# A linear-attention and token-mixing kernel: 20 of its 24 activation transposes moved from TensorE to DMA transposes

## The chip, the cores and the metric

One core of one Trainium2 chip runs the whole kernel. The metric is the device time of one launch in microseconds, lower is better. Five runs of the kernel before gave a median of 159.87 us (157.64 to 160.91).

## What is computed

The reference first runs a decayed linear attention over `r`, `k`, `v` (batch 4, 8 heads, 768 tokens, head width 48), then mixes the result, called x (4 x 768 x 384), across tokens and channels:

```python
for t in range(S):                       # per batch and head
    cur = einsum('bhd,bhe->bhde', u * k[t], v[t])
    y[t] = einsum('bhd,bhde->bhe', r[t], state + cur)
    state = w * state + einsum('bhd,bhe->bhde', k[t], v[t])
...
theta = x @ w_theta
zr, zi = x * cos(theta), x * sin(theta)
u = x + einsum('ts,bsd->btd', w_tok_r, zr) + einsum('ts,bsd->btd', w_tok_i, zi)
out = u + maximum(u @ w_ch, 0)
```

Inputs and output are float32; inside, most products are taken in bfloat16.

## The kernel before

**The work.** The 768 tokens are cut into 6 chunks of 128; two chunks make a pair, and there are 3 pairs in a batch and 12 in all. I call them g0 to g11, g = 3 * batch + pair. The attention is done in chunked form (line 506, `attention`): k is scaled on GpSimd (POOL, L520), turned on TensorE (PE), scored against r (L543), masked on VectorE (DVE, L548); a running state S goes from chunk to chunk (L585, L593, L603, L613); the products with v and with S make y (L627, L632); and DVE adds a diagonal term to give x (L639), token-major, bfloat16, 128 partitions x 768 for a pair.

**The two matrices that are turned.** `theta` (L651) needs x with channels on the partitions, so x of a pair is turned block by block (six 128 x 128 blocks) into xT. ScalarE (ACT) then takes sin (L655) and cos (L658), and DVE and POOL multiply with x to give zr (L661) and zi (L664). When zr and zi of the three pairs of a batch are there, `mixing` (line 668) sums over all tokens: each output chunk takes 12 matmuls, issued as 4 parts of 3 (L683), and DVE adds x to give un (L689). `f` (L700) needs un with channels on the partitions, so un of a pair is turned in the same way into uT; DVE then makes `fin` (L704), and SyncE (SP) stores it (L708).

In the kernel before, `flips` (defined above L473) does both turns: six TensorE transposes against an identity into one PSUM bank (L473), and a copy of the 128 x 768 result into SBUF, on DVE (L261) or ACT (L259). xT, un, uT and fin each have two buffers. The turned r (RT) and k (KT) come from the same helper, and the token weights are turned in fp32 at L456; the change leaves these alone.

**What sets the order.** Nothing is ordered by hand. `P.add` records each task with the engines that may run it, a cost for each as (busy ns, latency ns), its reads and writes, and a priority; `Plan.order` (line 88) then simulates the five engines with these costs, and the order of starts that comes out is the order in which each engine's instructions are issued. Engines run their own list strictly in order. A task with two engines among its options goes where the plan has it done first. DMAs are tasks of SP: loads cost 1080 ns (k, v), 3500 ns (r of a batch) and so on with a latency of 2100 ns and have a priority of -1e6 plus their number; the output stores have (1000, 2000) and a priority of -2e6, ahead of every load that could start at the same moment:

```python
P.add({SP: (ns, 2100)}, lambda e: nc.sync.dma_start(out=dst, in_=src), wr=wr,
      prio=-1e6 + pos, name="load")
```

All loads but three tiny ones, and all stores, go through SP. Loads run ahead into ten staging tiles `ld` and two `r_f` tiles. On SP, a DMA also waits for the DMA issued eight before it, whose semaphore it takes over.

The plan counts PE instructions as `pe_op(ns)`, an extra latency of 215 ns, and a copy as `ev(n)`, ACT or DVE.

Of the kernel before, what the change touches and what calls it, by code (L numbers as in the profile page):

```python
# [16 lines left out]
BF16 = mybir.dt.bfloat16  # L17
# [3 lines left out]
PE, DVE, ACT, POOL, SP = "PE", "DVE", "ACT", "POOL", "SP"  # L21
# [167 lines left out]
def act_op(n, psum=True, ptr=False):  # L189
    return (n / 1.2 + (85 if psum else 100) + (90 if ptr else 0), 135)  # L190


def dve_op(n, rate=1.0):
    return (n / (0.96 * rate) + 70, 115)
# [6 lines left out]
def pe_op(ns):  # L201
    return (ns, 215)


@with_exitstack
def kernel(
    ctx: ExitStack,
    tc: tile.TileContext,
    r: bass.AP,
    k: bass.AP,  # L210
    v: bass.AP,
    w: bass.AP,
    u: bass.AP,
    moe_w_theta: bass.AP,
    moe_w_tok_r: bass.AP,
    moe_w_tok_i: bass.AP,
    moe_w_ch: bass.AP,
    out: bass.AP,
):
    nc = tc.nc  # L220
    P = build(ctx, tc, nc, r, k, v, w, u, moe_w_theta, moe_w_tok_r, moe_w_tok_i, moe_w_ch, out)
    ctx.enter_context(tc.manual_schedule())
    for t in P.order():
        t.fn(t.eng)


def build(ctx, tc, nc, r, k, v, w, u, moe_w_theta, moe_w_tok_r, moe_w_tok_i, moe_w_ch, out):
    B, H, S, D = r.shape
    HD = H * D
    C = 128  # L230
    NCH = S // C
    ND = HD // C
    Dp = 64
    HP = H // 2
    NP = NCH // 2
# [4 lines left out]
    P = Plan(SLOTS)  # L240
    banks = [ps.tile([C, n, 512], F32, name=f"bank{i}") for i, n in enumerate(SLOTS)]

    def dbl(tok):
        return banks[P.bank_of[tok]]

    def bank(tok):
        return banks[P.bank_of[tok]][:, 0]

    def bank16(tok):
        return banks[P.bank_of[tok]].bitcast(BF16)[:, 0]  # L250

    def ring(n, shape, dt, nm):
        return [sb.tile(shape, dt, name=f"{nm}{i}") for i in range(n)]
# [3 lines left out]
    def copy(e, dst, src):  # L257
        if e == ACT:
            nc.scalar.activation(dst, src, Act.Copy)  # L259
        else:  # L260
            eng_of[e].tensor_copy(dst, src)  # L261
# [17 lines left out]
    wS = sb.tile([C, HP, 2 * D], F32, name="wS")  # L279
    uw = sb.tile([C, HP, 2], BF16, name="uw")  # L280

    NL, NR, NK, NV = 10, 2, 4, 5
    Ls = ring(NL, [C, 2, H, Dp], F32, "ld")
    r_fs = ring(NR, [C, H, NCH * D], F32, "r_f")
    Rws = ring(1, [C, NCH, H, Dp], BF16, "Rw")
# [10 lines left out]
    zrs = ring(2, [C, NCH, HD], BF16, "zr")  # L296
    zis = ring(2, [C, NCH, HD], BF16, "zi")
    sins = ring(2, [C, 2, HD], BF16, "sin")
    xTs = ring(2, [C, 2 * ND, C], BF16, "xT")
    uns = ring(2, [C, 2, HD], BF16, "un")  # L300
    uTs = ring(2, [C, 2 * ND, C], BF16, "uT")
    fins = ring(2, [C, 2, HD], F32, "fin")
    Wth = sb.tile([C, ND, HD], BF16, name="Wth")
    Wch = sb.tile([C, ND, HD], BF16, name="Wch")
# [127 lines left out]
    def L2(i):  # L432
        return [("L", i, 0), ("L", i, 1)]
# [34 lines left out]
    def flips(dst, blocks, tok, prio, rd, wr, name, opts, src=lambda t: t):  # L468
        n = len(blocks)

        def go(e):
            for i, s in enumerate(blocks):
                nc.tensor.matmul(bank16(tok)[:, i * C:(i + 1) * C], s, ident,  # L473
                                 is_transpose=True, start=(i == 0), stop=(i == n - 1))
        P.add({PE: pe_op(56 * n)}, go, rd=rd + ["ident"], acq=[(tok, 1)], prio=prio, name=name)
        P.add(opts, lambda e: copy(e, dst, src(
            bank16(tok)[:, :n * C].rearrange("p (a c) -> p a c", a=n))),
            use=[tok], wr=wr, prio=prio, name=name + "ev")

    EV = {ACT: None, DVE: None}  # L480

    def ev(n):
        return {ACT: act_op(n), DVE: dve_op(n, 2.0)}
# [22 lines left out]
    def attention(b, pr, base):  # L506
        RT, x, zr, zi = RTs[b % 2], xs[b % 2], zrs[b % 2], zis[b % 2]
        zj = b % 2
        g = b * NP + pr
        pb = base  # L510
# [13 lines left out]
        if b == 0:  # L524
# [9 lines left out]
            rd=L2(iv) + ["tables done"], wr=[kv_], prio=pb + 1, name="vcast")  # L534

        for c in range(2):
            tk, cc = ("A", g, c), 2 * pr + c

            def scores(e, tk=tk, c=c, cc=cc):
                for hp in range(HP):  # L540
# [6 lines left out]
                  prio=pb + 2, mode=1, name="scores")  # L547
# [7 lines left out]
            rd=[kT] + rt_keys, wr=[kP], prio=pb + 2.5, lock=True, name="PD")  # L555
# [35 lines left out]
        def outer0(e):  # L591
            if S_in:
# [5 lines left out]
              rd=[kK, kv_] + ([S_in, "ident"] if S_in else []), acq=[(tS, 1)], prio=pb + 2.2,  # L598
              name="outer")
# [10 lines left out]
        if not last:  # L610
            P.add({PE: pe_op(170)}, lambda e: outer(1, False), rd=[kK, kv_], use=[tS], wr=[tS],
                  prio=pb + 2.4, name="outer")
# [6 lines left out]
        def outputs(e):  # L619
            for c in range(2):  # L620
# [17 lines left out]
        xk = [("x", zj, pr)]  # L638
# [1 line left out]
            x[:, 2 * pr:2 * pr + 2], dbl(ty)[:, :, :HD], yd),  # L640
            use=[ty], rd=[ky], wr=xk, prio=pb + 5, name="x")

        xT, sn = xTs[g % 2], sins[g % 2]
        flips(xT, [x[:, 2 * pr + t, dk * C:(dk + 1) * C] for t in range(2) for dk in range(ND)],
              ("TX", g), pb + 6, xk, [("xT", g % 2)], "xT", ev(6 * C))
        th = ("th", g)

        def theta(e):
            for t in range(2):
                for dk in range(ND):  # L650
                    nc.tensor.matmul(dbl(th)[:, t, :HD], xT[:, ND * t + dk, :], Wth[:, dk, :],  # L651
                                     start=(dk == 0), stop=(dk == ND - 1))
        P.add({PE: pe_op(980)}, theta, rd=[("xT", g % 2), ("Wth", 0), ("Wth", 2)],
              acq=[(th, 2)], prio=pb + 7, name="theta")
        P.add({ACT: act_op(2 * HD)}, lambda e: nc.scalar.activation(  # L655
            sn, dbl(th)[:, :, :HD], Act.Sin), use=[th], rd=["tables done"],
            wr=[("sin", g % 2)], prio=pb + 7, name="sin")
        P.add({ACT: act_op(2 * HD, True, True)}, lambda e: nc.scalar.activation(  # L658
            dbl(th)[:, :, :HD], dbl(th)[:, :, :HD], Act.Sin, bias=pi2), use=[th],
            wr=[th], rd=["pi2"], prio=pb + 7.1, name="cos")  # L660
        P.add({DVE: dve_op(2 * HD)}, lambda e: nc.vector.tensor_mul(  # L661
            zr[:, 2 * pr:2 * pr + 2], dbl(th)[:, :, :HD], x[:, 2 * pr:2 * pr + 2]), use=[th],
            rd=xk, wr=[("zr", zj, pr)], prio=pb + 8, name="zr")
        P.add({POOL: pool_op(2 * HD, 1.9)}, lambda e: nc.gpsimd.tensor_mul(  # L664
            zi[:, 2 * pr:2 * pr + 2], x[:, 2 * pr:2 * pr + 2], sn),
            rd=xk + [("sin", g % 2)], wr=[("zi", zj, pr)], prio=pb + 8, lock=True, name="zi")

    def mixing(b, pr, base):
        x, zr, zi = xs[b % 2], zrs[b % 2], zis[b % 2]
        zj = b % 2  # L670
        zk = [("zr", zj, o) for o in range(NP)] + [("zi", zj, o) for o in range(NP)]
        g = b * NP + pr
        un, uT, fin = uns[g % 2], uTs[g % 2], fins[g % 2]
        pb = base
        for t in range(2):
            to = 2 * pr + t
            tm = ("mx", b, to)
            for part in range(4):
                def mix(e, tm=tm, to=to, part=part):
                    WT, z = ((WrT, zr), (WiT, zi))[part // 2]  # L680
                    for j in range(3):
                        so = 3 * (part % 2) + j
                        nc.tensor.matmul(bank(tm)[:, :HD], WT[:, so, to * C:(to + 1) * C],  # L683
                                         z[:, so], start=(part == 0 and j == 0),
                                         stop=(part == 3 and j == 2))
                P.add({PE: pe_op(490)}, mix, rd=zk + [(n, to) for n in ("WrT", "WiT")],
                      acq=[(tm, 1)] if part == 0 else [], use=[] if part == 0 else [tm],
                      wr=[] if part == 0 else [tm], prio=pb + t - 0.01 * part, name="mix")
            P.add({DVE: dve_op(HD)}, lambda e, tm=tm, t=t, to=to: nc.vector.tensor_add(  # L689
                un[:, t], bank(tm)[:, :HD], x[:, to]), use=[tm],  # L690
                rd=[("x", zj, pr)], wr=[("un", g % 2, t)], prio=pb + t - 100, name="un")
        flips(uT, [un[:, t, dk * C:(dk + 1) * C] for t in range(2) for dk in range(ND)],
              ("TU", g), pb + 2, [("un", g % 2, t) for t in range(2)], [("uT", g % 2)], "uT",
              ev(6 * C))
        tf = ("f", g)

        def chan(e):
            for t in range(2):
                for dk in range(ND):
                    nc.tensor.matmul(dbl(tf)[:, t, :HD], uT[:, ND * t + dk, :], Wch[:, dk, :],  # L700
                                     start=(dk == 0), stop=(dk == ND - 1))
        P.add({PE: pe_op(980)}, chan, rd=[("uT", g % 2), ("Wch", 0), ("Wch", 2)],
              acq=[(tf, 2)], prio=pb + 2, name="f")
        P.add({DVE: dve_op(2 * HD)}, lambda e: nc.vector.scalar_tensor_tensor(  # L704
            fin, dbl(tf)[:, :, :HD], 0.0, un, op0=Alu.max, op1=Alu.add),
            use=[tf], rd=[("un", g % 2, t) for t in range(2)], wr=[("fin", g % 2)],
            prio=pb - 98, name="fin")
        P.add({SP: (1000, 2000)}, lambda e: nc.sync.dma_start(  # L708
            out=out[b, 2 * pr * C:(2 * pr + 2) * C, :].rearrange("(t p) n -> p t n", p=C),
            in_=fin), rd=[("fin", g % 2)], wr=[("out", g)], prio=-2e6, name="out")  # L710
# [3 lines left out]
    load_r(0, 2)  # L714
    heads(0, 0)
    attention(0, 0, 5)
    attention(0, 1, 15)
    attention(0, 2, 25)
    token_weights(range(0, 3), 40)
    load_r(1)  # L720
# [3 lines left out]
    for b in range(1, B + 1):  # L724
        if b < B:
            if b > 1:
                load_r(b)
                heads(b, 100 * b)
            for pr in range(NP):
                attention(b, pr, 100 * b + 5 + 10 * pr)  # L730
        for pr in range(NP):
            mixing(b - 1, pr, 100 * (b - 1) + 150 + 10 * pr)
# [31 lines left out]
```

## Time and profile before

| what | value |
|---|---|
| median of 5 runs | 159.87 us |
| the profiled execution, its own time | 159.87 us |
| its span in the trace | 158.2 us |
| DVE, ACT, POOL busy | 109.3, 76.5, 75.8 us |
| HBM read, written | 20.06 MB, 4.72 MB |

The span is the stretch that the trace covers; 1.67 us of the execution's time lie outside it. In the profile, a row of a group gives line, engine, operation, output and inputs with their shapes, the count, then busy time in us and the mean ns of one, then how long the engine sat idle just before these instructions and what ended that. "L473 <-ident,x" are the transposes of x, "L473 <-ident,un" those of un. Times of "DMA to landing" run from the issue on SP to the semaphore.

Three parts of the run matter below: the start (to about 42 us: weights, batch 0), the middle (42 to 96 us: batches 1 and 2, while k and v still stream in), and the end (from 96 us: no more loads, only stores).

### The profile page before, as it was taken

What the parts mean: (1) busy time and instruction counts of PE and PEld (TensorE: products, weight loads), DVE (VectorE), ACT (ScalarE), POOL (GpSimd) and SP (SyncE); (2) the same over time, 40 slices, a digit from 0 to 9 for tenths busy, and PEclk for the clock granted to TensorE, in tenths of its full rate; (3) what the DMA queues carried; (4) which work ended last, traced back from release to release, by engine and by line L of the source; (5) the groups of instructions that cost most, each with busy time, mean ns of one, the idle gap of its engine ahead of it and who ended that gap; (6) DMA issues with size and microseconds to landing.
All of it is one profiled execution on the core that took longest, in us unless ns stands there. A gap on an engine that the chain in (4) does not pass through costs nothing.

```text
span 158.2 us, 3653 instructions
## 1 busy us (share of the span) xinstructions
PE 133.7 (85%) x1491; PEld 94.0 (59%) x1491; DVE 109.3 (69%) x158; ACT 76.5 (48%) x119; POOL 75.8 (48%) x61
## 2 busy tenths in 40 slices
PE   4077695599999999999889929999999999999950
PEld 1056564368787767669656717668567676566620
DVE  5196898812723999969999657667996975555540
ACT  3987238349887547558735184516317445000000
POOL 7000731669994846957599766910712442100000
PEclk9999999959999999999999999999999999999995
DMA  4999999999799999999999940202200022021022
GB/s 150 264 227 183 163 276 397 367 393 366 246 180 167 159 205 192 163 160 266 264 192 195 157 77 0 102 9 92 100 3 4 0 102 98 5 99 70 30 99 99
DMA packets 59962, 25.00 MB, mean 158 GB/s; under 512 B 50473, under 2 KB 58410, under 8 KB 59946
## 3 DMA queue, kind: packets, MB, share of 16 engines
q1 hardware_dynamic: 59920, 24.78, 74.5%
q8 instruction: 11, 0.18, 0.6%
q14 instruction: 5, 0.04, 0.1%
q10 hardware_dynamic: 26, 0.00, 0.0%
HBM read 20.06 MB, written 4.72 MB: 157 GB/s over the span
## 4 chain that ended last, share of the span: by engine, by line
PE 56%; DVE 21%; DMA 7%; SPq 7%; issue 3%; ACT 2%; POOL 1%; ACTq 1%; DVEq 0%; POOLq 0%
PE bank L683 23%; PE bank L473 8%; PE bank L700 7%; SPq L404 7%; PE bank L651 5%; DVE mAT L548 5%; PE bank L456 4%; DMA ld<-in_k_dram 4%; DMA ld<-in_v_dram 4%; DVE zr L661 3%; DVE PD L553 2%; PE bank L632 2%; PE bank L543 2%; DVE fin L704 2%; PE bank L627 2%
## 5 line engine op out<-in xcount | busy, mean ns | idle before, releaser
L683 PE MATMUL bank<-zi,WiT 128*128 128x384 bf16 x144 | 29.7, 326 | 0.0
L683 PE MATMUL bank<-zr,WrT 128*128 128x384 bf16 x144 | 29.2, 326 | 0.0
L548 DVE TENSOR_TENSOR mAT<-bank,mask 128x1024 bf16<-128x1024 f32 x24 | 28.8, 1216 | 0.1
L664 POOL TENSOR_TENSOR zi<-x,sin 128x768 bf16<-128x768 bf16 x12 | 20.6, 1720 | 15.7 <-ACT sin L655 15.7
L520 POOL TENSOR_TENSOR Kw<-ld,wpinv 128x768 bf16<-128x768 f32 x10 | 18.6, 1866 | 19.2 <-DMA ld<-in_k_dram 19.2
L568 POOL TENSOR_TENSOR yd<-dg,vb 128x768 bf16<-128x768 f32 x12 | 17.6, 1475 | 20.7 <-ACT dg L259 16.5
L651 PE MATMUL bank<-Wth,xT 128*128 128x384 bf16 x72 | 14.5, 340 | 4.2 <-DVE xT L261 2.8
L492 POOL TENSOR_TENSOR Rw<-r_f,wpow 128x576 bf16<-128x576 f32 x12 | 16.6, 1406 | 2.8 <-DMA r_f<-in_r_dram 2.8
L689 DVE TENSOR_TENSOR un<-bank,x 128x384 bf16<-128x384 f32 x24 | 13.3, 553 | 6.7 <-PE bank L683 6.7
L639 DVE TENSOR_TENSOR x<-bank,yd 128x768 bf16<-128x768 f32 x12 | 11.4, 954 | 8.2 <-PE bank L632 8.2
L683 PEld LDWEIGHTS <-WiT 128*128 128x128 bf16 x144 | 12.9, 98 | 7.1
L683 PEld LDWEIGHTS <-WrT 128*128 128x128 bf16 x144 | 12.8, 97 | 7.0
L259 ACT ACTIVATE vb<-ld 128x768 bf16<-128x768 f32 x12 | 10.1, 845 | 13.5 <-DMA ld<-in_v_dram 13.2
L704 DVE SCALAR_TENSOR_TENSOR fin<-bank,un 128x768 f32<-128x768 f32 x12 | 11.5, 957 | 6.0 <-PE bank L700 6.0
L655 ACT ACTIVATE sin<-bank 128x768 bf16<-128x768 f32 x12 | 9.8, 813 | 11.4 <-PE bank L651 5.8
L661 DVE TENSOR_TENSOR zr<-bank,x 128x768 bf16<-128x768 f32 x12 | 11.4, 951 | 4.3 <-ACT bank L658 4.3
L259 ACT ACTIVATE RT<-bank 128x768 bf16<-128x768 bf16 x16 | 12.0, 815 | 4.7 <-PE bank L473 4.7
L700 PE MATMUL bank<-Wch,uT 128*128 128x384 bf16 x72 | 13.7, 326 | 0.7 <-DVE uT L261 0.7
L651 PEld LDWEIGHTS <-xT 128*128 128x128 bf16 x72 | 7.1, 100 | 9.2 <-DVE xT L261 3.2
L543 PE MATMUL bank<-RT,KT 64*128 64x128 bf16 x192 | 9.8, 229 | 2.1 <-ACT KT L259 0.6
L658 ACT ACTIVATE bank<-bank,pi 128x768 f32<-128x768 f32 x12 | 10.5, 874 | 0.0
L473 PE MATMUL bank<-ident,Rw 128*128 128x128 bf16 x96 | 8.5, 246 | 1.9 <-DVE Rw L492 1.8
(79 smaller groups left out, 211.3 us busy)
## 6 DMA issues: line engine op xcount, KB each, us to landing
ld<-in_k_dram SPq DMA_DIRECT2D x24, 192.0 KB, 5.6
ld<-in_v_dram SPq DMA_DIRECT2D x24, 192.0 KB, 5.2
out_dram<-fin SPq DMA_DIRECT2D x12, 384.0 KB, 2.6
r_f<-in_r_dram SPq DMA_DIRECT2D x3, 1152.0 KB, 9.7
ld<-in_moe_w_tok_r_dram SPq DMA_DIRECT2D x6, 384.0 KB, 7.5
ld<-in_moe_w_tok_i_dram SPq DMA_DIRECT2D x6, 384.0 KB, 8.5
r_f<-in_r_dram SPq DMA_DIRECT2D x2, 576.0 KB, 4.5
ld<-in_moe_w_theta_dram SPq DMA_DIRECT2D x1, 384.0 KB, 5.0
```

Source lines behind the costliest of these rows:

```text
L259: nc.scalar.activation(dst, src, Act.Copy)
L473: nc.tensor.matmul(bank16(tok)[:, i * C:(i + 1) * C], s, ident, is_transpose=True, start=(i == 0), stop=(i == n - 1))
L492: eng_of[e].tensor_mul(Rw[:, :, 2 * hp:2 * hp + 2, :D].transpose([0, 2, 1, 3]), rf[:, 2 * hp:2 * hp + 2, :].rearrange("p h (n d) -> p h n ...
L520: eng_of[e].tensor_mul(Kw[:, :, :, :D].rearrange("p a h d -> p (a h) d"), Ls[ik][:, :, :, :D].rearrange("p a h d -> p (a h) d"), wpinv.rea ...
L548: P.add({DVE: dve_op(8 * C)}, lambda e, tk=tk, c=c: nc.vector.tensor_mul(mAT[:, c].rearrange("p a h t -> p (a h) t"), dbl(tk).rearrange("p ...
L568: P.add({POOL: pool_op(2 * HD, 1.7)}, lambda e: nc.gpsimd.tensor_mul(yd.rearrange("p a (h d) -> p (a h) d", h=H), wide(dg, D), vb.rearrang ...
L651: nc.tensor.matmul(dbl(th)[:, t, :HD], xT[:, ND * t + dk, :], Wth[:, dk, :], start=(dk == 0), stop=(dk == ND - 1))
L661: P.add({DVE: dve_op(2 * HD)}, lambda e: nc.vector.tensor_mul(zr[:, 2 * pr:2 * pr + 2], dbl(th)[:, :, :HD], x[:, 2 * pr:2 * pr + 2]), use= ...
L664: P.add({POOL: pool_op(2 * HD, 1.9)}, lambda e: nc.gpsimd.tensor_mul(zi[:, 2 * pr:2 * pr + 2], x[:, 2 * pr:2 * pr + 2], sn), rd=xk + [("si ...
L683: nc.tensor.matmul(bank(tm)[:, :HD], WT[:, so, to * C:(to + 1) * C], z[:, so], start=(part == 0 and j == 0), stop=(part == 3 and j == 2))
L700: nc.tensor.matmul(dbl(tf)[:, t, :HD], uT[:, ND * t + dk, :], Wch[:, dk, :], start=(dk == 0), stop=(dk == ND - 1))
L704: P.add({DVE: dve_op(2 * HD)}, lambda e: nc.vector.scalar_tensor_tensor(fin, dbl(tf)[:, :, :HD], 0.0, un, op0=Alu.max, op1=Alu.add), use=[ ...
```

## The change

```diff
-    NL, NR, NK, NV = 10, 2, 4, 5
+    NL, NR, NK, NV, NXT = 10, 2, 4, 5, 2
...
+    def turn(dst, src, prio, rd, wr, name):
+        P.add({SP: (750, 2100)}, lambda e: nc.sync.dma_start_transpose(out=dst, in_=src),
+              rd=rd, wr=wr, prio=prio - 2e6, name=name)
...
-        flips(xT, [x[:, 2 * pr + t, dk * C:(dk + 1) * C] for t in range(2) for dk in range(ND)],
-              ("TX", g), pb + 6, xk, [("xT", g % 2)], "xT", ev(6 * C))
+        if b == 0:
+            flips(xT, [x[:, 2 * pr + t, dk * C:(dk + 1) * C] for t in range(2)
+                       for dk in range(ND)], ("TX", g), pb + 6, xk, [("xT", g % NXT)], "xT",
+                  ev(6 * C))
+        else:
+            turn(xT, x[:, 2 * pr:2 * pr + 2].rearrange("p t n -> p (t n)"), pb + 6, xk,
+                 [("xT", g % NXT)], "xT")
...
+        uk = [("un", g % 2, t) for t in range(2)]
+        if g == B * NP - 1:
+            flips(uT, [un[:, t, dk * C:(dk + 1) * C] for t in range(2) for dk in range(ND)],
+                  ("TU", g), pb + 2, uk, [("uT", g % NXT)], "uT", ev(6 * C))
+        else:
+            turn(uT, un.rearrange("p t n -> p (t n)"), pb + 2, uk, [("uT", g % NXT)], "uT")
```

xT of g3 to g11 (9) and uT of g0 to g10 (11) are now made by one DMA each, issued on SP, that turns a 128 x 768 bfloat16 tile SBUF to SBUF as six 128 x 128 blocks. TensorE still turns x of batch 0 and un of g11. The ring sizes stay two. The plan is told that such a DMA holds SP for 750 ns and lands 2100 ns later, and that it goes ahead of a load that could start at the same moment. Since the plan makes the order anew, other tasks move on every engine too; their number stays as it was, and only the 20 x 6 TensorE transposes and the 20 copies are gone.

More of the change, by code (lines that the diff above doesn't have):

```diff
@@ L298, in build @@
     sins = ring(2, [C, 2, HD], BF16, "sin")
-    xTs = ring(2, [C, 2 * ND, C], BF16, "xT")
+    xTs = ring(NXT, [C, 2 * ND, C], BF16, "xT")
     uns = ring(2, [C, 2, HD], BF16, "un")
-    uTs = ring(2, [C, 2 * ND, C], BF16, "uT")
+    uTs = ring(NXT, [C, 2 * ND, C], BF16, "uT")
     fins = ring(2, [C, 2, HD], F32, "fin")
@@ L478, in flips @@
             use=[tok], wr=wr, prio=prio, name=name + "ev")
-    EV = {ACT: None, DVE: None}
+    def turn(dst, src, prio, rd, wr, name):
+        P.add({SP: (750, 2100)}, lambda e: nc.sync.dma_start_transpose(out=dst, in_=src),
+              rd=rd, wr=wr, prio=prio - 2e6, name=name)
     def ev(n):
@@ L641, in attention @@
             use=[ty], rd=[ky], wr=xk, prio=pb + 5, name="x")
-        xT, sn = xTs[g % 2], sins[g % 2]
-        flips(xT, [x[:, 2 * pr + t, dk * C:(dk + 1) * C] for t in range(2) for dk in range(ND)],
-              ("TX", g), pb + 6, xk, [("xT", g % 2)], "xT", ev(6 * C))
+        xT, sn = xTs[g % NXT], sins[g % 2]
+        if b == 0:
[5 more added lines that the diff above has]
+                 [("xT", g % NXT)], "xT")
         th = ("th", g)
@@ L652, in theta @@
                                      start=(dk == 0), stop=(dk == ND - 1))
-        P.add({PE: pe_op(980)}, theta, rd=[("xT", g % 2), ("Wth", 0), ("Wth", 2)],
+        P.add({PE: pe_op(980)}, theta, rd=[("xT", g % NXT), ("Wth", 0), ("Wth", 2)],
               acq=[(th, 2)], prio=pb + 7, name="theta")
@@ L672, in mixing @@
         g = b * NP + pr
-        un, uT, fin = uns[g % 2], uTs[g % 2], fins[g % 2]
+        un, uT, fin = uns[g % 2], uTs[g % NXT], fins[g % 2]
         pb = base
@@ L691, in mixing @@
                 rd=[("x", zj, pr)], wr=[("un", g % 2, t)], prio=pb + t - 100, name="un")
-        flips(uT, [un[:, t, dk * C:(dk + 1) * C] for t in range(2) for dk in range(ND)],
-              ("TU", g), pb + 2, [("un", g % 2, t) for t in range(2)], [("uT", g % 2)], "uT",
-              ev(6 * C))
+        uk = [("un", g % 2, t) for t in range(2)]
[4 more added lines that the diff above has]
+            turn(uT, un.rearrange("p t n -> p (t n)"), pb + 2, uk, [("uT", g % NXT)], "uT")
         tf = ("f", g)
@@ L701, in chan @@
                                      start=(dk == 0), stop=(dk == ND - 1))
-        P.add({PE: pe_op(980)}, chan, rd=[("uT", g % 2), ("Wch", 0), ("Wch", 2)],
+        P.add({PE: pe_op(980)}, chan, rd=[("uT", g % NXT), ("Wch", 0), ("Wch", 2)],
               acq=[(tf, 2)], prio=pb + 2, name="f")
```

## The prediction, made before the changed kernel was run

> **What bounds the kernel now.** I read the page's 40 slices first, then busy time by stage, then the chain of waits, then TensorE's (PE's) timeline, then the DMAs by stage.
>
> The slices (3.96 us each; a 9 is 90% or more) show PE full from about slice 11 to slice 38, while the DMA row is full only up to slice 24:
>
> ```profile
> span 158.2 us, 3653 instructions
> PE   4077695599999999999889929999999999999950
> DMA  4999999999799999999999940202200022021022
> ```
>
> The stages say it in us: PE is busy 49.63 of 54 us in the middle and 39.91 of 40 after it, while VectorE (DVE, third pair of numbers), ScalarE (ACT) and GpSimd have air. The DMA share over 1 in the middle is overlap; it says "full".
>
> ```profile
> 42.00:96.00 54.00, 49.63 (x628) 36.15 (x629) 41.84 (x53) 33.06 (x53) 39.93 (x25) 1.00 1.14 178
> 96.00:136.00 40.00, 39.91 (x456) 27.21 (x453) 30.92 (x41) 17.15 (x27) 16.09 (x10) 1.00 0.14 51
> ```
>
> So a microsecond of PE work saved from 42 us on is a microsecond gained, as long as nothing makes PE wait. The chain of waits (start, us, what) shows what the turns and their neighbours cost PE. Six transposes take 0.34 us (the groups' 219 ns each counts overlap):
>
> ```profile
> 146.54 0.34 PE bank L473 x6
> 146.87 0.97 PE bank L683 x6
> 147.85 0.97 PE bank L700 x6
> ```
>
> The one long PE wait of the middle comes through DMA. ACT runs in order; its cast of v stood 3.62 us for a v load, the sine of the pair queued behind it, and PE's next theta waited 2.81 us for what came after:
>
> ```profile
> 90.41 0.84 ACT L259 ACTIVATE vb<-ld 128x768 bf16<-128x768 f32 x1 [3.62 <-DMA ld<-in_v_dram]
> ```
>
> ```profile
> 94.37 1.15 PE L651 MATMUL bank<-Wth,xT 128*128 128x384 bf16 x6 [2.81 <-DVE xT L261]
> ```
>
> Last, the DMAs: KB each and median us from issue to landing, in the middle and then at the end. The same store lands in 5.4 us among the loads and in 2.4 without them: a backlog of 3.0 us stands in the queues. SyncE (SP) gives out a 192 KB load every 1.1 us, two in about 2.3:
>
> ```profile
> ld<-in_v_dram SPq DMA_DIRECT2D x18, 192.0 KB, 5.2
> ld<-in_k_dram SPq DMA_DIRECT2D x17, 192.0 KB, 5.4
> out_dram<-fin SPq DMA_DIRECT2D x3, 384.0 KB, 5.4
> r_f<-in_r_dram SPq DMA_DIRECT2D x1, 1152.0 KB, 7.2
> ```
>
> ```profile
> out_dram<-fin SPq DMA_DIRECT2D x9, 384.0 KB, 2.4
> ```
>
> ```profile
> 62.85 2.22 SPq L404 DMA_DIRECT2D ld<-in_v_dram  x2
> 65.17 2.27 SPq L404 DMA_DIRECT2D ld<-in_k_dram  x2
> ```
>
> **Step 1, what goes.** 20 turns leave PE: 20 x 0.335 us (chain) = 6.7 us, all of it at or after 52 us, where PE is full. Gain: 6.7. The copies that go are 10 on DVE (0.55 us each) and 10 on ACT (0.81), 5.5 and 8.1 us; neither engine ends the run while PE is full, so I count them at nothing (below that they were waits of the turns themselves, which step 2 replaces). The PSUM banks that the turns held come free as well; no row shows PE waiting for a bank after 42 us, so nothing for that.
>
> **Step 2, what comes: 20 DMAs and their landing time L, from SP's issue to the semaphore.** Before, a turn took 0.34 on PE and 0.55 or 0.81 for the copy. No row shows a transpose by DMA. It moves 192 KB, as a k load does, and by its shape in 128 x 6 runs of 256 bytes, near the k load's 1024 runs of 192. At the end of the run L lies between the quiet store, 2.4, and the crowded one, 5.4; I take the middle, 3.9. In the middle of the run it queues behind loads: between the v load's 5.2 and the r load's 7.2; I take 6.2. The ends without any reason to choose are 2.4 for both (the queue happens to be empty) and 5.4 / 7.2.
>
> What L costs depends on the PE work that stands between the maker of x or un and the user of its turn in the changed program's order. With 0.49 for a part of mix, 0.97 for theta or f, 0.74 for y, 0.34 and 0.45 for the turns of r and k, 0.40 for scores with its change of tiling, 0.18 for outer and diag, and less the DVE add that comes first (x 0.96, un 0.56), I get this cover in us:
>
> - Middle: xT of g3 4.05, g4 5.5, g5 2.3, g6 5.5, g7 5.3, g8 about 4.3 (its add waits for GpSimd's yd); uT of g4 4.3, and 5.7 or more for g0 to g3. For g5: after y stand two r turns, theta, an r turn, two k turns and two outers, 3.25, less 0.96.
> - End: xT of g9 4.66, g10 4.8, g11 3.4; uT of g5 3.5, g6 and g7 7 or more, g8 1.4, g9 3.36, g10 3.36. For g8: after its last mix stand f of g7 and two parts of mix, 1.95, less 0.56.
>
> PE works in order, so while theta or f waits, the mix, scores and y behind it wait too, and DVE's masks and adds with them; that is why a wait counts in full. A late theta also makes its zr late, and on DVE x of g11 stands behind zr of g9; I charge nothing for such handing on. A wait is L minus cover, less any earlier wait that falls inside the same cover. Middle at 6.2: g3 2.15; xT g4 0.7; g5 3.9 - 0.7 = 3.2; g6 0.7; g7 0.9 - 0.7 = 0.2; uT g4 1.9 - 0.2 = 1.7; xT g8 inside that. Sum 8.65. End at 3.9: uT g5 0.4; xT g11 0.5; uT g8 2.5; uT g9 0.5; uT g10 inside that. Sum 3.9. Together 12.55. The wait at uT g8 includes one that is there at any L: theta of g11 now has only 1.95 us behind it before the mix that needs zr, against sin, cos and zr in about 2.7.
>
> At the ends: L = 2.4 everywhere leaves 0.1 + 1.0 = 1.1. L = 5.4 / 7.2 gives 12.65 + 10.7 = 23.4.
>
> **Step 3, what the transposes do to SP and the loads.** SP works in order, and a transpose waits there for DVE; behind it stand k and v loads and stores of fin. The r load stands behind them too. GpSimd issues no DMA, and its own list only waits later where x or k comes later. Nine transposes stand ahead of the v load that ACT waited for at 90.41. By runs, a transpose costs the queues 768/1024 of a load's 1.1 us, 0.83; nine make that load 7.5 us later. PE comes there later by its own waits until then (2.15 + 0.7 + 3.2 + 0.7 = 6.75) less nine turns saved (3.0): 3.75. So ACT's cast could hold the sine up to 3.75 us more than it does now; but while SP waits for x, the queues drain. Bounds 0 and 3.75; I take half, 1.9. The last k load has more room: its scaling ran at 99.8, its turn on PE at 108.4.
>
> **Two statements of the Trainium skill, beside the sum.** The row is the quiet 384 KB store, 2.4 us. "Advanced Engine Details and Errata", section X-Bar Transpose (TRN2), says that transposing DMAs are as fast as ordinary ones; with 2.4 and 5.3 for L and nothing for step 3, step 2 would cost 6.25, and the kernel would stay at 159.4. "VectorE: DVE Perf Modes", section The three transpose paths, gives 1309 ns for a 128 x 128 bfloat16 block by DMA against 390 ns on TensorE. The rows have 0.06 us a block on PE (0.34 / 6). Six blocks in a row would be 7.9 us, an estimate from that page; by it, with the 3.0 of backlog, step 2 would cost about 50 us, and the kernel would take about 203. No row of this trace decides between the pages, and the sum uses neither.
>
> **Sum.** -6.7 + 12.55 + 1.9 = +7.75. The profiled execution took 159.87 (its span 158.2 and 1.67 around it), which is also the median of the five runs. 159.87 + 7.75 = 167.6 us.
>
> **Rivals.**
> - *The transposes land at once, and the kernel is faster.* For it: at the end the queues are 14% busy, and in the middle SP now waits for DVE ahead of each transpose, which lets the backlog run off. Against: 42 to 96 us is DMA-full, at two loads in 2.3 us. With 2.4 everywhere: 159.87 - 6.7 + 1.1 = 154.3. It decides from L of about 4.2 in the middle and 2.6 at the end downward: there the waits are 0.15 + 1.9 + 1.2 = 3.25, and the time is 156.4.
> - *Gain and waits cancel.* L near 5.1 and 3.0: waits of 1.05 + 2.8 + 0.8 + 1.6 = 6.25, and 159.4. For it: the k load is as large, and the covers are mostly 3 to 5 us.
> - *The queues become the bound.* A transpose that holds all 16 queues for T us in place of 0.83. Against: equal bytes. For: nothing in the trace shows a DMA that writes across partitions in pieces. Nine of them cost 9T - 3.75 at the v cast in place of 1.9; at T = 2, 14.25, and 180.
> - *The change does nothing*: excluded, the changed order has 20 DMA transposes on SP and 120 fewer TensorE transposes.
>
> **How the numbers follow.** Forecast (step 2 and 3 between about 10 and 21 us, 163 to 174): 0.42. Cancel: 0.2. Faster rival: 0.2. Queue-bound, or L beyond the upper ends: 0.18. From 154.3 as the floor, half of the faster rival lies above 155.5. Above, the upper ends of steps 2 and 3 give 159.87 - 6.7 + 23.4 + 3.75 = 180.3, with half of the last case below it. So 155.5 to 180 leaves out 0.1 on each side; the forecast's own range is 163 to 174. About 2% is what a measurement of this kernel can tell from no change (its runs spread from 157.64 to 160.91): faster than that 0.2, within 0.2, slower 0.6.
>
> **What would show it.** The landing times of the new rows on SP at the two stages (6.2, 3.9); the transposes of x down from 72 to 18 and those of un from 72 to 6; PE waits before L651 in the middle, the largest at g5's theta, and before L700 for g8 and g9 at the end; PE's idle time up by about 14 us; the DMA row full for longer than slice 24. The forecast is wrong if L at the end is under 3, or if the middle's queues are no longer full when a transpose is issued; and upward, if a transpose holds the queues for more than a load does.

## The result, and the profile after

| | median, us | against the kernel before |
|---|---|---|
| before, 48 runs | 159.69 | |
| changed, 27 runs | 160.57 | ratio 1.0099, 95% interval 1.0072 to 1.0126 |

The change costs 1.0%. I had forecast 167.6. The sign was right and the size was not: if the 6.7 us of work went in full, they met some 8.3 us of new waits (6.7 + 1.6), where I had priced 14.45. The profiled executions are single ones, of 159.87 and 159.71 us, and TensorE's granted clock in their last 22 us was 0.92 before and 0.98 after, so their spans (158.2, 158.0) do not show the 1%. The ratio comes from undisturbed runs alone, here and in all tables below, so it is not the quotient of the two medians.

The page of the changed kernel, the span and two rows of the 40 slices:

```profile
span 158.0 us, 3421 instructions
...
PE   4067585569899987997579999679999999699960
...
DMA  4999999999899899999999999998023375522522
```

TensorE (PE) now has its main holes in slices 19 to 21, 26, 27 and 35, and the DMA row is full up to slice 28, where it was full up to slice 23. Busy time by stage (after the length of the stage, the first pair of numbers is PE):

```profile
42.00:96.00 54.00, 48.50 (x597) 33.41 (x595) 40.04 (x52) 26.95 (x41) 36.70 (x24) 1.00 1.16 189
96.00:136.00 40.00, 36.57 (x372) 22.66 (x371) 28.39 (x37) 15.17 (x24) 18.46 (x12) 1.00 0.65 112
```

In these 94 us, which held 89.54 us of PE work before, there are 85.07 now. Over the whole run PE's busy time fell from 133.7 to 127.1 us. The work went; the time did not.

How long do the new DMAs take? The DMA view of the changed kernel, first for 42 to 96 us, then for 118 to 158 us (count, median us from issue to landing), then the line of min/median/max from the view of tile xT and from that of uT:

```profile
xT<-x SPq DMA_TRANSPOSE x5, 4.0
uT<-un SPq DMA_TRANSPOSE x4, 3.2
```

```profile
uT<-un SPq DMA_TRANSPOSE x5, 3.5
xT<-x SPq DMA_TRANSPOSE x3, 3.1
```

```profile
DMA to landing us min/median/max: 2.8/3.8/4.7
```

```profile
DMA to landing us min/median/max: 2.7/3.2/4.2
```

None took the 6.2 that I had used for the middle. So PE waits for a landing in four places only, 4.5 us in all. PE's timeline of the changed kernel, the four rows with such a wait in brackets and the one wait that is there at any landing time (the run without turns, below, has the same 1.26):

```profile
76.75 1.15 PE L658 MATMUL bank<-Wth,xT 128*128 128x384 bf16 x6 [1.83 <-DMA xT<-x]
...
91.73 1.15 PE L658 MATMUL bank<-Wth,xT 128*128 128x384 bf16 x6 [0.21 <-DMA xT<-x]
...
103.77 1.15 PE L710 MATMUL bank<-Wch,uT 128*128 128x384 bf16 x6 [2.27 <-DMA uT<-un]
...
111.66 1.15 PE L710 MATMUL bank<-Wch,uT 128*128 128x384 bf16 x6 [0.21 <-DMA uT<-un]
...
136.53 0.48 PE L690 MATMUL bank<-zr,WrT 128*128 128x384 bf16 x2 [1.26 <-DVE zr L668]
```

What grew most lies on another engine. ScalarE's (ACT) waits for v loads (us in total, times, longest), before and then changed:

```profile
ACT vb L259 <- DMA ld<-in_v_dram: 13.2, 8, 3.6
```

```profile
ACT vb L259 <- DMA ld<-in_v_dram: 22.9, 9, 4.6
```

And the last v load leaves SyncE (SP) at 101.27, where the last two left from 87.75 on before. SP's timeline, before and then changed:

```profile
87.75 3.04 SPq L404 DMA_DIRECT2D ld<-in_v_dram  x2
```

```profile
101.27 0.57 SPq L404 DMA_DIRECT2D ld<-in_v_dram  x1
```

PE's timeline also has waits for k and v: 0.63 and 0.48 us for a scaled k, 0.93 for a cast v, 2.0 together, at 59, 81 and 61 us. So two suspects: PE waiting for landings, or k and v arriving later. A third is that the plan's new order is simply worse.

### The profile page after: what moved, and what is told of

Read it like the earlier page. It is cut to its first block, busy times and chain, and to the rows that moved or that the text cites. A ratio compares the mean times of both kernels' runs of the same rounds, so it can differ in the third digit from the quotient of the medians.

```text
span 158.0 us, 3421 instructions
## 1 busy us (share of the span) xinstructions
PE 127.1 (80%) x1371; PEld 85.2 (54%) x1371; DVE 104.1 (66%) x150; ACT 68.5 (43%) x106; POOL 74.8 (47%) x61
## 4 chain that ended last, share of the span: by engine, by line
PE 43%; DMA 26%; POOL 11%; SPq 7%; DVE 4%; issue 4%; ACT 2%; POOLq 0%; DVEq 0%; ACTq 0%
PE bank L690 20%; DMA r_f<-in_r_dram 11%; SPq L404 7%; DMA uT<-un 7%; PE bank L710 6%; POOL Rw L494 5%; PE bank L658 4%; DMA ld<-in_k_dram 4%; DMA ld<-in_v_dram 3%; PE bank L456 3%; PE bank L473 3%; POOL Kw L522 3%; PE bank L545 2%; POOL yd L570 2%; PE bank L634 1%
## 5 line engine op out<-in xcount | busy, mean ns | idle before, releaser
L690 PE MATMUL bank<-zi,WiT 128*128 128x384 bf16 x144 | 28.7, 326 | 0.0
L671 POOL TENSOR_TENSOR zi<-x,sin 128x768 bf16<-128x768 bf16 x12 | 19.7, 1640 | 11.5 <-ACT sin L662 11.5
L658 PE MATMUL bank<-Wth,xT 128*128 128x384 bf16 x72 | 13.7, 326 | 3.7 <-DMA xT<-x 2.0
L658 PEld LDWEIGHTS <-xT 128*128 128x128 bf16 x72 | 6.6, 97 | 9.1 <-DMA xT<-x 3.6
L710 PEld LDWEIGHTS <-uT 128*128 128x128 bf16 x72 | 6.7, 98 | 8.7 <-DMA uT<-un 3.7
```

## The experiments

In the runs that leave the turn out or do not use it, the 20 products concerned (theta or f) read blocks of the weights in place of xT and uT. The work of each matmul stays the same, but these products no longer wait for x or un either. In each table row the ratio is to the kernel before, measured on the same chip, with its 95% interval.

**No turn at all, in the changed order.**

```diff
-        P.add({SP: (750, 2100)}, lambda e: nc.sync.dma_start_transpose(out=dst, in_=src),
+        P.add({SP: (750, 2100)}, lambda e: None,
```

> The changed kernel in its own order, with the 20 DMA transposes left out and not replaced: theta and f of the pairs concerned read blocks of the weights instead of xT and uT (so x and un are not turned at all there). Three theories of where the 6.7 us of TensorE work that the change saves went. Landing (TensorE waits for the transposes to land): the waits before theta and f vanish, 1.8 + 2.3 + 0.2 + 0.2 us in the changed trace, and what they hold up: about 155. Queue (k and v loads are held up behind the transposes): the casts of v on ScalarE wait as in the kernel before (13 us and not 23): about 154 to 156. Order (the new order is worse by itself, above all theta of g11 coming late before the mix that needs its zr): about 158 to 160.

**All transposes issued, nobody waits for them.** The edit is only in the operand of theta and f:

```diff
-    nc.tensor.matmul(dbl(th)[:, t, :HD], xT[:, ND * t + dk, :], Wth[:, dk, :],
+    nc.tensor.matmul(dbl(th)[:, t, :HD],
+                     xT[:, ND * t + dk, :] if b == 0 else Wth[:, dk, t * C:(t + 1) * C], Wth[:, dk, :],
```

> The changed kernel with all 20 DMA transposes issued at their places, but with theta and f of those pairs reading blocks of the weights, as in the run without turns: nothing waits for a transpose, and the load on SyncE and on the queues stays (the turned data is not used). Landing: as fast as the run without turns, about 155. Queue: as slow as the changed kernel, about 160, with the v casts on ScalarE waiting about 23 us. Order: 158 to 160 in both.

**The kernel before without its 20 turns, in its own order.** In `flips`, the transposes and the copy of those pairs are not emitted.

> The kernel before in its own order, with the same 20 turns left out (120 transposes on TensorE, 20 copies) and not replaced; theta and f of those pairs read blocks of the weights. All theories: the 6.7 us of TensorE work go, less what the one long wait for a v load keeps: 152 to 154. Landing and queue: no faster than the changed kernel without its turns, within 1 us. Order: 3 us or more faster than that.

| run | us | ratio | interval |
|---|---|---|---|
| changed order, no turns | 152.89 | 0.9638 | 0.9602 to 0.9675 |
| changed order, turns issued and unread | 158.79 | 0.9991 | 0.9955 to 1.0027 |
| changed kernel (from above) | 160.57 | 1.0099 | 1.0072 to 1.0126 |
| old order, no turns | 156.56 | 0.9869 | 0.982 to 0.9919 |

This splits the result, with 1% at 1.59 us: leaving the turns out of the changed order gains 3.6%, 5.8 us, more than any of the theories had expected. Issuing the DMAs, with nobody waiting for one, gives 3.5% back, 5.6 us. Waiting for them (and for x and un) adds 1.1%, 1.7 us. So most of the loss is there before anyone waits for a landing, as the queue theory says. The order theory falls: the new order without turns is the faster of the two. The old one without turns gains only 1.3%, short of the 152 to 154 expected. Its wait at theta in the middle stays (2.66 us at 92.47; ACT's sine stood there behind a v cast that waited 3.58 us for its load); that this is the reason was not tested.

The split depends on what is taken out first, because the two losses overlap. In the changed kernel itself PE stands 4.5 us at landings and 2.0 us at k and v. Where the landing of g5's turn no longer stops PE (1.83 us at theta), PE runs on and waits 2.11 us for the next scaled k, where it had waited 0.48. So 1.7 us is what landing adds to the loss from the queue. What landing would cost by itself, with the loads in time, was not run.

What the issued DMAs hold up is seen when the two runs stand side by side. ACT's wait for v loads, without turns and then with unread ones:

```profile
ACT vb L259 <- DMA ld<-in_v_dram: 9.6, 7, 3.9
```

```profile
ACT vb L259 <- DMA ld<-in_v_dram: 21.2, 9, 3.7
```

And in the run with unread turns, PE stands for k and v themselves. PE's timeline, then GpSimd's, whose scaling of k waited for its load just before:

```profile
63.41 0.33 PE L587 MATMUL bank<-vb,Kw 128*128 128x96 bf16 x4 [1.17 <-ACT vb L259]
...
83.03 1.03 PE L473 MATMUL bank<-ident,Kw 128*128 128x128 bf16 x8 [2.11 <-POOL Kw L522]
```

```profile
81.17 1.80 POOL L522 TENSOR_TENSOR Kw<-ld,wpinv 128x768 bf16<-128x768 f32 x1 [3.89 <-DMA ld<-in_k_dram]
```

Neither PE wait is in the run without turns. ACT's total wait is no measure of the price: with plain copies, the next experiment, it is 18.5 us at nearly no price.

**What of a DMA transpose delays the loads: SP standing before it until x or un is made, SP's 1.2 us to issue it, or its packets in the queues?** Four more forms of the unread run:

```diff
 # plain copy of the same 192 KB, same place, same wait
+  nc.sync.dma_start(out=dst.rearrange("p a c -> p (a c)"), in_=src)
 # transposes a constant tile: no wait for x or un
+  nc.sync.dma_start_transpose(out=dst, in_=Wth.rearrange("p o c -> p (o c)")[:, :6 * C])
 # the same, issued by ACT on its own queue
+  nc.scalar.dma_start_transpose(out=dst, in_=Wth.rearrange("p o c -> p (o c)")[:, :6 * C])
 # half of each transpose
+  nc.sync.dma_start_transpose(out=dst[:, :3], in_=src[:, :3 * C])
```

> As the run whose 20 transposes nobody waits for (158.8), with each transpose replaced by an ordinary DMA of the same 192 KB from x or un into the same tile, at the same place on SyncE, waiting for the same DVE add (nothing is turned, theta and f of those pairs read weight blocks). The 5.9 us between that run and the one without turns (152.9) come from one of three: SyncE standing in order before a transpose until DVE has made x or un, with loads behind it (head of line); SyncE's own 1.2 us to issue a transpose; the transposes' packets in the DMA queues. Head of line: 158 to 159, as before. Issue time or packets of the transpose: 153 to 154.5, since an ordinary DMA of 128 rows issues in about 0.4 us.

> As the run whose 20 transposes nobody waits for, but each transposes a constant tile (the theta weights), so SyncE does not wait for DVE before it; place, size, issue and packets stay (x and un are not turned, theta and f of those pairs read weight blocks). Head of line: as fast as without turns, 152.5 to 154. Issue time or packets: 157.5 to 159.

> As the run with transposes of a constant tile, but issued by ScalarE on its own DMA queue, at the place in ScalarE's list where SyncE's would have been made; SyncE gives out loads and stores alone (x and un are not turned, theta and f read weight blocks). If SyncE's issue time is what costs: 153 to 155, less where ScalarE, now with some 24 us more, is late. If the packets on the 16 engines cost: as the constant-tile run on SyncE, 157 to 159. Head of line: no statement on this one beyond 153 to 154.

> As the run whose 20 transposes nobody waits for, with each of them cut to half its width (three of six blocks, 96 KB; the turned data is not used, theta and f of those pairs read weight blocks). If the transposes' packets on the 16 DMA engines cost, by their number: halfway between no turns (152.9) and whole ones (158.8), 155 to 156.5, and the last v load leaves SyncE at about 96 to 98 us of the trace, between 91 and 103. If each transpose costs a fixed time whatever its size: 157.5 to 159.

| run | us | ratio | interval |
|---|---|---|---|
| plain copies | 154.0 | 0.9673 | 0.9625 to 0.972 |
| half transposes | 156.2 | 0.9812 | 0.9747 to 0.9877 |
| transposes of a constant, from ACT | 157.79 | 0.9916 | 0.9877 to 0.9955 |
| transposes of a constant, from SP | 157.8 | 0.9937 | 0.99 to 0.9975 |

The head of line is not it: the plain copies wait for the same x and un in the same places, and cost only 0.35% over no turns; and transposes that wait for nothing still cost 3.0%. SP's time to issue is not it alone: with ACT issuing them, SP gives out loads alone, and the time is the same. (ACT's own 24 us of issue could have cost as much as SP saved; I cannot exclude that.) And a half transpose holds SP as long as a whole one, at least 1.18 against 1.21 us, but costs half: 0.9812 lies midway between 0.9638 and 0.9991. SP's hold in the run with halves (ns, smallest, median, largest):

```profile
L481 SPq DMA_TRANSPOSE uT<-un x11: 1179/1200/1949, 51.0 to 139.8; - x11
```

What remains is the room that the transposes take in the DMA queues, and the DMA view shows it directly at the end, where no load runs. From 118 to 158 us, packets, MB and the packets' time as a share of the 16 DMA engines' 40 us: in the run with no turns (6 stores), in the changed kernel (6 stores, 8 transposes), with plain copies (6 stores, 6 copies), with halves (6 stores, and packets for 6.8 half transposes):

```profile
q1 hardware_dynamic: 1632, 2.36, 16.2%
```

```profile
q1 hardware_dynamic: 8032, 3.93, 41.2%
```

```profile
q1 hardware_dynamic: 2496, 3.54, 24.3%
```

```profile
q1 hardware_dynamic: 4476, 3.03, 24.8%
```

Less the stores, that is 1.25 us of all 16 engines for a transpose, 0.54 for a plain copy of the same tile and 0.5 for a half transpose.

SP's timeline shows what this does to the loads. The last v load leaves, in the runs with no turns (the second of two issues, at about 90.4), plain copies, half transposes and transposes of a constant:

```profile
89.28 2.29 SPq L404 DMA_DIRECT2D ld<-in_v_dram  x2
```

```profile
95.36 0.58 SPq L404 DMA_DIRECT2D ld<-in_v_dram  x1
```

```profile
98.71 0.57 SPq L404 DMA_DIRECT2D ld<-in_v_dram  x1
```

```profile
101.19 0.58 SPq L404 DMA_DIRECT2D ld<-in_v_dram  x1
```

Ten of the new DMAs stand ahead of that load. They delay it by 5.0, 8.3 and 10.8 us: about 0.5 us for a plain copy and 1.1 for a transpose of the same 192 KB. The price in total time is 0.6, 2.8 and 4.7 us (ratios times 159): by these three points some 4 us of delay are free, and the rest costs about 0.7 us for each us. The half transposes delay the load by more than half (0.8 us each; 98.71, past the 96 to 98 expected), so a part of the delay goes with the number of transposes and not with their packets. SP's hold may be that part; this was not separated.

PE's timelines show the price where it is paid. From 42 us on, the waits that the run with no turns does not have add up to 0.9 us with plain copies, 2.7 with halves, 5.0 with constants from SP and 6.1 with whole unread transposes, against prices of 0.6, 2.8, 4.7 and 5.6. All but 0.3 (plain copies) and 0.9 (unread) of that ends with a scaled k, a cast v, or a zr whose cosine stood behind a v cast. The largest, for plain copies, halves and constants, is for the same scaled k:

```profile
78.31 0.62 PE L473 MATMUL bank<-ident,Kw 128*128 128x128 bf16 x8 [0.49 <-POOL Kw L523]
```

```profile
79.61 1.03 PE L473 MATMUL bank<-ident,Kw 128*128 128x128 bf16 x8 [2.36 <-POOL Kw L523]
```

```profile
81.09 1.03 PE L473 MATMUL bank<-ident,Kw 128*128 128x128 bf16 x8 [3.55 <-POOL Kw L523]
```

**Transposes only after the loads.** x of batch 3 and un of g5 to g10, 9 turns, the plan told (1250, 1550):

> A full kernel: DMA transposes only where the loads are over, x of batch 3 and un of g5 to g10 (9 turns), TensorE turns the rest; the plan is told (1250, 1550), the issue and landing that the trace shows at the end. Nine turns are 3.0 us of TensorE. If the cost of the change lies in the middle among the loads (all three forms of the queue theory): 155.5 to 157.5. If the order is what counts, anything from 155 to 160.

158.47 us, ratio 0.9875 (0.9812 to 0.9938). The median lies above the 155.5 to 157.5 expected; the ratio, on a base of 159, gives 157.0. Nine turns hold 3.0 us of PE work; 2.0 of it is kept (1.0 to 3.0 by the interval). Away from the loads the change pays.

**What the plan is told.** Full kernels; the only edit is one or two pairs of numbers. I had asked whether a better told plan puts loads and turns where they cost less.

```diff
-        P.add({SP: (750, 2100)}, lambda e: nc.sync.dma_start_transpose(out=dst, in_=src),
+        P.add({SP: (1250, 2600)}, lambda e: nc.sync.dma_start_transpose(out=dst, in_=src),
...
-        P.add({SP: (ns, 2100)}, lambda e: nc.sync.dma_start(out=dst, in_=src), wr=wr,
+        P.add({SP: (ns, 4000)}, lambda e: nc.sync.dma_start(out=dst, in_=src), wr=wr,
```

> The changed kernel with one edit: the plan is told (1250, 2600) for a transpose in place of (750, 2100), near what the trace shows for its issue and landing in the middle. Landing: the plan puts more TensorE work between a turn and its user, the waits shrink: 157 to 158.5. Queue: the loads get later by the same amount, no change, 159.5 to 160.5. Order: no clear direction, 158 to 161.

> The changed kernel with the plan told (1250, 1600) for a transpose: the same landing as before (2850 after issue) and only a longer hold of SyncE, 1250 in place of 750. With (1250, 2600) the kernel took 155.8. If the plan gained by putting the loads later where they really are: 155 to 157. If it gained by more cover for the landing: 159 to 160.5, as the changed kernel.

> The changed kernel with the plan told (750, 3100): the same landing after issue as in the run with (1250, 2600), 3850, and the short hold of SyncE as in the change. If the plan gained by cover for the landing: 155 to 157. If by putting the loads later: 158.5 to 160.5.

> A full kernel: the changed one with (1250, 2600) for a transpose and the latency of every load told as 4000 in place of 2100, so that it lands in the plan about 5 us after issue, as it does in the traces. If ScalarE's and GpSimd's waits in order for v and k are what is left: 153 to 155.5. If they were not on the path: no change from 155.8, within 1 us.

> The kernel before, all turns on TensorE, with only the loads' latency told as 4000 in place of 2100. If the 154.2 of the run with both edits comes from the order of the loads' users and not from DMA transposes: 153 to 156 here too. If the DMA transposes earn it once the plan knows what they cost: 157.5 to 159.5.

> The changed kernel with (1250, 1600) for a transpose and 4000 for the loads' latency, the two edits that helped alone. If they add: 153 to 154.2. If the landing told matters once the loads are out of the way: 154.5 to 156.5, behind the run with (1250, 2600) and 4000.

| turns | transpose told as | loads' latency told as | us | ratio | interval |
|---|---|---|---|---|---|
| DMA | (750, 2100), the change | 2100 | 160.57 | 1.0099 | 1.0072 to 1.0126 |
| DMA | (750, 3100) | 2100 | 160.71 | 1.0056 | 1.0003 to 1.011 |
| DMA | (1250, 2600) | 2100 | 155.8 | 0.9843 | 0.9815 to 0.987 |
| DMA | (1250, 1600) | 2100 | 155.33 | 0.9754 | 0.97 to 0.9808 |
| DMA | (1250, 2600) | 4000 | 154.2 | 0.9698 | 0.9647 to 0.9748 |
| DMA | (1250, 1600) | 4000 | 162.53 | 1.0216 | 1.0161 to 1.027 |
| TensorE | | 4000 | 159.08 | 1.0039 | 1.0002 to 1.0076 |

Three of these beat both kernels, the best of them the kernel before by 3.0%. The first of them, (1250, 2600), was a surprise: no theory had it under 157, and the queue theory expected no change. That a longer hold puts the loads in the plan where they really are was thought of after it. The rows (1250, 1600) and (750, 3100), run to test it, fit: with the hold alone told as 1250 the kernel gains, with the landing alone it does not. The kernel before with the loads told later gains nothing, so that edit by itself does not give the 3.0%. Whether another order of it, with the turns on TensorE, would was not tried. But the last DMA row upsets the simple reading: the two edits that helped alone are together the slowest. In the best version PE hardly waits for landings; in the worst it waits for uT three times, 4.8 us in all, of which 2.98 near the end. Waits of the best one, then PE's timeline of the worst:

```profile
ACT vb L259 <- DMA ld<-in_v_dram: 6.0, 3, 2.7
...
PE bank L658 <- DMA xT<-x: 0.3, 1, 0.3
PE bank L710 <- DMA uT<-un: 0.3, 1, 0.3
```

```profile
137.57 2.10 PE L710 MATMUL bank<-Wch,uT 128*128 128x384 bf16 x6 [2.98 <-DMA uT<-un]
```

Too little cover, with the landing told too short, would explain it, but the run with (1250, 1600) and 2100 was told the same landing, and PE waits 0.9 us for uT there. Orders from slightly different numbers differ by up to 5%, so one kernel for each pair does not prove that the number told was the cause.

## Why the prediction was wrong

- **Step 1, the work saved: right.** 6.7 us forecast. PE's busy time fell by 6.6 us over the whole profile, by 4.5 in the 94 us from 42 on, and without any turn the changed order gains 5.8 us over before. That it is a PE-bound kernel holds only with the loads in time: in the old order, the same work left out gains 2.1 us. One reading was wrong, at no cost: PE does wait for a bank after 42 us, 0.51 us at 78.75 for a score whose bank `fin` had to release, and 0.52 in the changed kernel.
- **Step 2, the landing: the step that failed.** I took L = 6.2 in the middle and 3.9 at the end, and priced the waits at 12.55. L was 3 to 4 in both, 4.7 at most; PE stood 4.5 us at landings, and waiting for them cost 1.7 us over unread transposes. With the measured medians my own covers leave 1.7 us in the middle (g5) and 2.2 at the end, 3.9 in place of 12.55, so the size of L is most of the miss. The covers account for the rest: uT of g4 has no wait at these medians, and waited 2.27. The 6.2 came from the landing of loads, 5.2 and 7.2, in the belief that a transpose queues behind a full backlog. Two things in the changed trace speak against that: loads issued after a transpose take SP 0.5 us and not 1.1, so the queue had room again, which I had named as a sign of being wrong; and the landing of the loads themselves fell, to 4.7 and 4.9 medians. I had named that drain as an argument for the fast rival, and left it out of the middle value. The places were right where a wait was left: theta of g5 (1.83; 3.2 forecast), the mix that needs zr of g11 (1.26; about 0.8). uT of g4 waited 2.27 (1.7 forecast). xT of g3 and g4 (2.15, 0.7 forecast) show no wait at all, xT of g6 0.21 (0.7) and uT of g5 0.21 (0.4).
- **Step 3, the loads: right mechanism, size too small.** I took 0.83 us of queue for a transpose and a price of 1.9 us within 0 to 3.75. It was 1.1 us, and the price 5.6 with unread transposes. The bound was too low because I looked at one place, the v cast at 90 us. PE also waits for scaled k and for v at other pairs (2.11, 1.17 us above; 0.63, 0.93, 0.48 in the changed kernel), and each of these is a loss of its own. It partly makes up for step 2: 12.55 + 1.9 was forecast, 1.7 + 5.6 measured.
- **The rivals.** "Gain and waits cancel" came out, at 160.57 against the 159.4 worked out for it, but in part by another road: it had all 6.25 us of waits at the landings, where PE stands 4.5 us and the zr of g11 another 1.26, and it had nothing for k and v, where most of the loss is by the unread run. The queue rival named that place, with T = 1.1 where it wanted 2 for 180 us. By its own formula, 9T - 3.75 is 6.2 us at T = 1.1, near the 5.6 measured, but that is luck: the 3.75 holds 6.75 us of landing waits ahead of that v cast, of which 1.83 came; with that alone the formula gives about 11.
- **The skill's two statements.** "Advanced Engine Details and Errata", X-Bar Transpose (TRN2), has transposing DMAs as fast as ordinary ones. For the landing that is near: 4.3 and 3.3 us for unread transposes of x and un in the middle, 3.8 and 3.4 for plain copies in their place. For the queue it is not: 1.1 us of delay for each against 0.5, 1.25 us of the engines' time against 0.54. The 1309 ns for a block in "VectorE: DVE Perf Modes", The three transpose paths, does not add up over six blocks here: a whole transpose, issue and landing included, took 2.7 to 4.7 us.

## What to carry to other kernels

A transpose moved to DMA leaves TensorE but not the chip: ask first what else is in the queues, and price it by the queue time that it takes from the loads, not by its own landing alone. To tell the two apart, issue the DMA and let nobody read it: what is lost then is the queue's, and the rest is what landing adds to it. And where a planner orders the work, give it the measured hold and landing of a new operation, then measure several orders; here the same change lies between -3.0% and +2.2%.

## What the runs showed of the hardware that was not expected

- Issuing one 128 x 768 bfloat16 DMA transpose holds SP for 1.21 us where nothing is in its way (smallest of 20), against 0.38 for a 384 KB store.
- A transpose of 192 KB delays the loads behind it by 1.1 us, as much as SP's spacing of 192 KB loads among themselves (1.1 us), though a plain SBUF-to-SBUF copy of the same tile delays them by 0.5. Where no load runs, the packets of one take 1.25 us of all 16 engines, those of the copy 0.54. In packets: 16,000 more on the queue for 20 transposes, 800 each, against 144 for a plain copy (62,800 and 59,920 in all).
- A last v load that is 5 us late went with a price of 0.6 us and one that is 11 us late with 4.7, which suggests, but does not show, that the run-ahead in the staging tiles was worth about 4 us.
- Half the width of a transpose takes 0.5 us of the engines' time in place of 1.25, but holds SP as long: 1.18 us at least, against 1.21.
